# Seven products of sums in place of eight, in the second layer's first product, with second products between them

## The chip, the core and the metric

The kernel runs on one NeuronCore of a Trainium2 chip. The metric is the time of one execution on the device in microseconds (us). Matrix products run on TensorE (PE in the profile, its weight loads PEld), elementwise work on VectorE (DVE), ScalarE (ACT) and GpSimd (POOL); transfers are issued from SyncE's queue (SP).

## What is computed

A linear attention with decay over 2 x 768 tokens of 8 heads of 64, then two feed-forward layers over the 1,536 tokens. The second layer, which the change is about, is a 512 x 2048 product, a leaky relu and a 2048 x 512 product. The weights come as float64.

```python
state = gamma[None, :, None, None] * state + np.einsum('bhd,bhe->bhde', k[:, :, t], v[:, :, t])
y[:, :, t] = scale * np.einsum('bhd,bhde->bhe', q[:, :, t], state)
...
xn = x / rms * rms_g
g = xn @ w_gate
silu = g * (1.0 / (1.0 + np.exp(-g)))
val = xn @ w_val
return (silu * val @ w_out).astype(np.float32)
...
h = x @ w_in
g = np.maximum(0.01 * h, h)
return (g @ w_out).astype(np.float32)
```

## The kernel before

The tokens are cut into three blocks of 512 (`BLOCKS`, numbered 0 to 2), the first layer's 1,536 inner features into 12 blocks of 128, the second's 2,048 into 16. Every operand of a large product is kept as a high part and a low part (`split`, L412 and L413, for what is computed; the conversion of the weights, L362 to L376), and a product is taken as high by high, low by high and high by low. So `product_t` (L407), which multiplies a weight block of 512 x 128 by a token block, is 4 parts of the 512 times 3, that is 12 matrix instructions of 128 x 128 by 128 x 512. A second product (`proj`, L453, in the first layer, `down`, L514, in the second) is 12 too: four output banks times 3.

**Weights.** A block of weights is called a unit: `g`, `v`, `o` of the first layer, `i` and `p` of the second. `fetch` (L342) loads its float64 bits (512 KB), and six steps convert it: three instructions on ACT (L362, L363, L373) and five on DVE (L381, L382, L366, L372, L376). The units come in the order of use, `i` and `p` in turn. There are places for 12 units, and for 10 more once the attention's buffers are given back. After each step of the program `convert` puts 4 or 8 of these conversion steps into it; `need` puts in all that a step's weights still lack.

**The first stage.** The attention goes over 12 chunks of 128 tokens. Per chunk there are scores `sc` (L148), their decay `a` on DVE (L154), an outer product `u` (L164) and heads `y` (L181, L192). Per pair of chunks a norm follows: `tot` on PE (L227), `na` on DVE (L236), a Newton iteration of 13 small instructions on POOL (`nr`, `nt`, L241 to L246), `bc` on PE (L252), then `xg` (L269) and `xl` (L275) on DVE and `xh` (L270) on ACT. The first chunks go through ahead of the first layer, in an order written out by hand; the rest is put between the steps of the first layer on blocks 0 and 1, at a rate worked out from the number of tasks left (`attention`, `per`, `credit`).

**The first layer.** In three groups of four feature blocks (`G1`), for each token block: `gate`, `val` and, one step late, `proj`.

**The second layer.** In three groups of 6, 5 and 5 feature blocks (`G2`), for each of the three token blocks: `up` (the first product, 12 matrix instructions, then a leaky relu `la` on ACT, L501, and the split), and `down` two steps late, which sums over the group's blocks into four banks; `evac` adds them to `y2acc` (L532) and, in the last group, writes them out (L535).

A scheduler takes the program as written, places tiles and sets the order on each engine; only the first part of the attention has an order written out by hand. Banks for products come from a pool of four (`ps`, `bank`), the accumulators of second products from four others (`ps_acc`); `scr` has 6 buffers of 128 x 512 for what comes out of the banks.

Of the kernel before, what the change touches and what calls it, by code (L numbers as in the profile page):

```python
# [23 lines left out]
G2 = [6, 5, 5]  # L24
UNITS = 12
UNITS2 = 10
# [4 lines left out]
EARLY_FETCH = 4  # L31
# [5 lines left out]
def chain_kernel(ctx: ExitStack, tc: tile.TileContext, qk_t, kv, w1, w2, mask, qdec, kdec, sdec, rms_g, ident, out):  # L37
# [244 lines left out]
    def attention(c0, due):  # L282
# [19 lines left out]
        for c in range(c0, NCHUNK + 1):  # L302
# [20 lines left out]
    slots = [[units, UNITS, set()]]  # L323
    wq = [(n + str(f), w1[f, :, i, :]) for f in range(NF1) for i, n in enumerate("gvo")]
    wq += [(n + str(f), w2[f, :, i, :]) for f in range(NF2) for i, n in enumerate("ip")]
    index = {key: i for i, (key, _) in enumerate(wq)}
    raw = {}
    fetched = [0]
    converting = []
    started = [0]  # L330

    def release(key, b):
        if b == NB - 1:
            for s in slots:
                s[2].discard(key)

    def fetch():
        if fetched[0] < min(len(wq), started[0] + RAWS):
            key, src = wq[fetched[0]]
# [4 lines left out]
    def start_unit():  # L344
        slot = next((s for s in slots if len(s[2]) < s[1]), None)
        if slot is None or started[0] == len(wq):
            return False
        key = wq[started[0]][0]
# [3 lines left out]
        slot[2].add(key)  # L352
        t = raw.pop(key)
        low, high = t[:, :, 0], t[:, :, 1]
        a = stage.tile([P, 512], F32, tag="a", name=f"wa_{key}")
# [3 lines left out]
        v = nc.vector  # L359
# [62 lines left out]
    def moe1(g, b, fs, steps):  # L422
# [40 lines left out]
        def evac(banks):  # L463
            if g == 0:
                acc[b] = xp.tile([P, 4, T], F32, tag=f"acc{BLOCKS[b]}", name=f"x2acc{b}")
            last = g == len(G1) - 1
            if last:
                x2h[b] = xp.tile([P, 4, T], F32R, tag=f"xh{BLOCKS[b]}", name=f"x2h{b}")
                x2l[b] = xp.tile([P, 4, T], F32R, tag=f"xl{BLOCKS[b]}", name=f"x2l{b}")
            for m in range(4):  # L470
# [5 lines left out]
                if last:  # L476
                    nc.scalar.activation(out=x2h[b][:, m, :], in_=dst, func=AF.Copy)
            if last:
                for m in range(4):
                    nc.vector.tensor_tensor(  # L480
                        out=x2l[b][:, m, :], in0=acc[b][:, m, :], in1=x2h[b][:, m, :].bitcast(F32), op=ALU.subtract
                    )

        for f in fs:
            steps.append((f"g{f}", b, lambda f=f: gate(f)))
            steps.append((f"v{f}", b, lambda f=f: val(f)))
            steps.append((f"o{f}", b, lambda f=f: proj(f)))

    acc2 = {}

    def moe2(g, b, fs, steps):
        T = BLOCKS[b]
        nt = T // P
        prods = {}

        def up(f):
            hb = bank(f"up{f}_{b}")[:, :T]
            product_t(hb, wt[f"i{f}"], x2h[b], x2l[b])
            release(f"i{f}", b)
            a = scratch(f"la{f}_{b}")[:, :T]  # L500
            nc.scalar.activation(out=a, in_=hb, func=AF.Prelu, alpha=0.01)  # L501
            prods[f] = split(a, f"g2_{f}_{b}", T)

        def down(f):
            if f == fs[0]:
                acc["b"] = acc_banks(f"y2_{g}_{b}", nt)
            h, l = prods.pop(f)
            w = wt[f"p{f}"]
            release(f"p{f}", b)
            for m in range(nt):  # L510
# [10 lines left out]
            if f == fs[-1]:  # L521
                evac(acc.pop("b"))

        def evac(banks):
            if g == 0:
                acc2[b] = xp.tile([P, nt, 512], F32, tag=f"acc{BLOCKS[b]}", name=f"y2acc{b}")
            for m in range(nt):
# [9 lines left out]
        for f in fs:  # L537
            steps.append((f"i{f}", b, lambda f=f: up(f)))
            steps.append((f"p{f}", b, lambda f=f: down(f)))


    def in_order(steps, late):

        order, held = [], []
        for s in steps:
            if s[0][0] in "op":
# [3 lines left out]
            while len(held) > late[s[0][0]]:  # L550
# [4 lines left out]
    for groups, moe in ((G1, moe1), (G2, moe2)):  # L555
        base = 0
        for g, n in enumerate(groups):
            for b in range(NB):
                moe(g, b, list(range(base, base + n)), steps)
# [143 lines left out]
```

## Time and profile before

| | us |
|---|---|
| median of 3 runs (646.64 to 647.08) | 646.76 |
| profiled execution, device time | 642.79 |
| span of the profiled execution, first to last instruction | 641.0 |
| TensorE busy in it | 621.2 |
| VectorE busy | 347.8 |
| ScalarE busy | 270.1 |
| GpSimd busy | 67.8 |

The profile is one execution. Its busy times are sums of instructions; a matrix instruction is shown with its pipeline's depth, so two that follow each other overlap in it, and the time of one in a stream is read from start to start. A wait is idle time of an engine with the instruction that ended it.

### The profile page before, as it was taken

The numbers are of one execution on the slowest core, as the hardware profiler recorded it, in microseconds if no ns is written. First come the engines' busy times: TensorE is split into PE (matmuls) and PEld (weight loads), VectorE is DVE, ScalarE is ACT, GpSimd is POOL, SyncE is SP. The second block draws the span as 40 slices with busy tenths as digits, with TensorE's granted clock in tenths as the row PEclk, the third lists the DMA queues.
The fourth block names the chain that finished last, engine by engine and source line by source line (L and its number), as shares of the span: only waits on it lengthen the run. The fifth ranks groups of instructions, "written<-read, shape, count | busy, mean of one in ns | idle before, by whom it ended". The sixth has DMA issues, their size and how long they took to land.

```text
span 641.0 us, 7899 instructions
## 1 busy us (share of the span) xinstructions
PE 621.2 (97%) x3074; PEld 512.2 (80%) x3074; DVE 347.8 (54%) x596; ACT 270.1 (42%) x482; POOL 67.8 (11%) x128
## 2 busy tenths in 40 slices
PE   7988789999999999999999999999999999999997
PEld 5866678878888888888888888888888888888886
DVE  3888997335999926992415996113951212222122
ACT  2556554426677513752314674325752222222220
POOL 4864545210000000000000000000000000000000
PEclk9998999999999999999999999999999999999999
DMA  9754444002545410532000443001300000001011
GB/s 336 267 208 162 147 151 132 1 1 67 164 137 180 132 44 26 172 132 67 0 1 0 146 150 100 1 0 34 130 2 0 1 0 1 2 0 66 0 66 65
DMA packets 15876, 52.74 MB, mean 82 GB/s; under 512 B 2144, under 2 KB 2272, under 8 KB 15840
## 3 DMA queue, kind: packets, MB, share of 16 engines
q1 hardware_dynamic: 15840, 52.25, 24.1%
q8 instruction: 24, 0.39, 0.2%
q14 instruction: 12, 0.10, 0.0%
HBM read 49.09 MB, written 3.15 MB: 81 GB/s over the span
## 4 chain that ended last, share of the span: by engine, by line
PE 89%; DVE 5%; POOL 2%; ACT 2%; issue 1%; DMA 1%; SPq 0%; POOLq 0%; DVEq 0%
PE up L407 20%; PE y L514 20%; PE x L453 15%; PE val L407 15%; PE gate L407 14%; PE y L192 1%; PE y L181 1%; DMA kdec_sb<-in_kdec 1%; PE sc L148 1%; PE u L164 1%; PE tot L227 1%; DVE wa_v L366 0%; DVE xl L275 0%; DVE wa_v L372 0%; DVE y2acc L532 0%
## 5 line engine op out<-in xcount | busy, mean ns | idle before, releaser
L407 PE MATMUL up<-x2h,w_i 128*128 128x512 f32 x384 | 94.8, 389 | 0.0
L501 ACT ACTIVATE la<-up 128x512 f32<-128x512 f32 x48 | 28.6, 596 | 151.5 <-PE up L407 151.4
L407 PEld LDWEIGHTS up<-x2h,w_i 128*128 128x128 f32 x384 | 72.1, 188 | 15.0
L407 PE MATMUL val<-xh,w_v 128*128 128x512 f32 x288 | 72.9, 395 | 3.7 <-DVE a L154 1.7
L407 PE MATMUL gate<-xh,w_g 128*128 128x512 f32 x288 | 72.6, 392 | 2.4 <-ACT w_g L373 1.2
L407 PEld LDWEIGHTS val<-xh,w_v 128*128 128x128 f32 x288 | 54.2, 190 | 15.7 <-ACT sq L206 1.8
L407 PEld LDWEIGHTS gate<-xh,w_g 128*128 128x128 f32 x288 | 53.6, 188 | 14.7 <-ACT w_g L373 2.8
L440 DVE TENSOR_TENSOR a<-val,t 128x512 f32<-128x512 f32 x36 | 24.7, 687 | 57.4 <-PE val L407 57.4
L407 PE MATMUL up<-x2l,w_i 128*128 128x512 f32 x192 | 51.3, 389 | 0.0
L413 DVE TENSOR_TENSOR g_1l<-la,g_1h 128x512 fp32r<-128x512 f32 x16 | 11.1, 692 | 62.9 <-ACT g_1h L412 62.9
L432 ACT ACTIVATE t<-gate 128x512 f32<-128x512 f32 x36 | 21.4, 594 | 54.8 <-PE gate L407 48.5
L407 PEld LDWEIGHTS up<-x2l,w_i 128*128 128x128 f32 x192 | 36.0, 188 | 7.5
L514 PE MATMUL y<-w_p,g_0h 128*128 128x512 f32 x128 | 39.4, 389 | 0.0
L514 PE MATMUL y<-w_p,g_1h 128*128 128x512 f32 x128 | 39.4, 389 | 0.0
L514 PE MATMUL y<-w_p,g_2h 128*128 128x512 f32 x128 | 39.4, 389 | 0.0
L407 PE MATMUL val<-xl,w_v 128*128 128x512 f32 x144 | 39.1, 394 | 0.0
L407 PE MATMUL gate<-xl,w_g 128*128 128x512 f32 x144 | 38.5, 389 | 0.0
L453 PE MATMUL x<-g_0h,w_o 128*128 128x512 f32 x96 | 33.4, 408 | 1.6 <-ACT g_0h L412 1.6
L413 DVE TENSOR_TENSOR g_0l<-la,g_0h 128x512 fp32r<-128x512 f32 x16 | 11.0, 690 | 41.9 <-ACT g_0h L412 41.9
L407 PEld LDWEIGHTS val<-xl,w_v 128*128 128x128 f32 x144 | 27.6, 192 | 5.8
L453 PE MATMUL x<-g_1h,w_o 128*128 128x512 f32 x96 | 31.6, 390 | 0.0
L407 PEld LDWEIGHTS gate<-xl,w_g 128*128 128x128 f32 x144 | 27.0, 188 | 5.7
(119 smaller groups left out, 1103.6 us busy)
## 6 DMA issues: line engine op xcount, KB each, us to landing
raw_i<-in_w SPq DMA_DIRECT2D x16, 512.0 KB, 3.8
raw_p<-in_w SPq DMA_DIRECT2D x16, 512.0 KB, 3.5
qkT<-in_qk_t SPq DMA_DIRECT2D x12, 512.0 KB, 4.7
kv<-in_kv SPq DMA_DIRECT2D x12, 512.0 KB, 5.9
raw_g<-in_w SPq DMA_DIRECT2D x12, 512.0 KB, 3.5
raw_v<-in_w SPq DMA_DIRECT2D x12, 512.0 KB, 3.4
raw_o<-in_w SPq DMA_DIRECT2D x12, 512.0 KB, 3.6
out<-y2acc SPq DMA_DIRECT2D x12, 256.0 KB, 2.1
```

What stands on the lines that cost most here:

```text
L148: nc.tensor.matmul(out=s["sc"][j][:, t], lhsT=k_[r, t], rhs=q_[r, t], start=True, stop=True)
L164: nc.tensor.matmul(out=u[:, t], lhsT=kd[:, t], rhs=s["kv"][:, 1, t], start=True, stop=True)
L181: nc.tensor.matmul(out=y[:, a * CH:(a + 1) * CH], lhsT=state[(c + 1) % 2][:, a, :], rhs=s["qs"][:, a, :], start=(a == 0), stop=False, skip ...
L192: nc.tensor.matmul(out=y[j * D:(j + 1) * D, a * CH:(a + 1) * CH], lhsT=s["kv"][:, 1, e:e + D], rhs=s["a"][j][:, a, :], start=not inter, st ...
L227: nc.tensor.matmul(out=nrm[cs]["tot"][:, i:i + 1], lhsT=part, rhs=ones, start=(j == 0), stop=(j == len(parts) - 1))
L407: nc.tensor.matmul(out=dst, lhsT=lhs, rhs=rhs, start=(n == 0), stop=(n == len(pairs) - 1))
L413: nc.vector.tensor_tensor(out=l[:, :T], in0=x, in1=h[:, :T].bitcast(F32), op=ALU.subtract)
L432: nc.scalar.activation(out=t, in_=gb, func=AF.Silu)
L440: nc.vector.tensor_tensor(out=a, in0=vb, in1=prods[f], op=ALU.mult)
L453: nc.tensor.matmul(out=acc["b"][m][:, :T], lhsT=lhs, rhs=rhs, start=(f == fs[0] and n == 0), stop=(f == fs[-1] and n == 2),)
L501: nc.scalar.activation(out=a, in_=hb, func=AF.Prelu, alpha=0.01)
L514: nc.tensor.matmul(out=acc["b"][m], lhsT=lhs, rhs=rhs, start=(f == fs[0] and n == 0), stop=(f == fs[-1] and n == 2),)
```

## The change

The second layer's first product on token blocks 1 and 2 is no longer computed block by block. Two neighbouring feature blocks f and e = f + 1 form a pair. Weights and tokens are cut into 2 x 2 parts (feature blocks f and e by two halves of the 512; the halves by token blocks 1 and 2), and the four results of 128 x 512 come from 7 products of sums of parts, where there were 8 products of parts (`quad`). A product of parts (`half`) is 2 parts times 3, that is 6 matrix instructions. The results build up in three banks, X, Z and Y. Between the products ACT copies what stands in X or Z into `scr` (`s1`, `s5`, `u2`), products go on adding into the same bank, and DVE adds the copies to the final banks (`added`). Block 0 keeps `up`.

The sums of weights (`s` units, two for a pair) are formed from the converted `i` units by four DVE instructions of 256 columns and split by two on ACT and two on DVE. The sums of tokens (`sums_of_x2`) are formed once, at the end of the first layer.

The order of steps in the second layer is written out: groups of four feature blocks (`G2`), per group four `up` with a second product behind each, then two pairs, with second products put between their seven products. Second products run up to one group behind. The last of a group's second products on block 1, and those on block 2, stand between the next group's steps; what is left at the end comes back to back.

Other edits: the places for units are 12, 2 for all kinds and 8 for the first layer's alone, which are given back at its end (22 in the first layer as before, 14 in the second where there were 22); `scr` has 5 buffers where it had 6; the conversion's buffer `a` has 3 where it had 2; four empty tasks stand ahead of the last norm's `bc`.

```diff
-G2 = [6, 5, 5]
+G2 = [4, 4, 4, 4]
-UNITS2 = 10
+UNITS2 = 2
+UNITS3 = 8
+HOLD = 5
...
+    stage_a = ctx.enter_context(tc.tile_pool(name="stage_a", bufs=3))
...
-    scr = ctx.enter_context(tc.tile_pool(name="scr", bufs=6))
+    scr = ctx.enter_context(tc.tile_pool(name="scr", bufs=5))
...
-                tasks += norm(due)
+                tasks += [lambda: None] * (4 if c == NCHUNK else 0) + norm(due)
...
+            converting.extend([
+                combine(e[:, two], e[:, one], e[:, two], ALU.add),
+                combine(e[:, one], a[:, one], e[:, one], ALU.subtract),
+                high_part(us[1], e),
+                combine(a[:, one], e[:, two], a[:, one], ALU.subtract),
+                combine(a[:, two], a[:, two], a[:, one], ALU.subtract),
+                high_part(us[0], a),
+                low_part(us[1], e, names[1]),
+                low_part(us[0], a, names[0]),
+            ])
...
+        def first(t, in0, in1, h, l):
+            nc.vector.tensor_tensor(out=t, in0=in0, in1=in1, op=ALU.subtract)
+            nc.scalar.activation(out=h, in_=t, func=AF.Copy)
+
+        def second(t, in0, in1, h, l):
+            nc.vector.tensor_tensor(out=l, in0=t, in1=h.bitcast(F32), op=ALU.subtract)
...
+        def half(dst, key, two, x, start):
...
+            for i, part in ((i, slice(k * P, (k + 1) * P)) for i, k in enumerate(ks)):
+                for lhs, rhs in ((w[:, 0, part], h[:, i]), (w[:, 1, part], h[:, i]), (w[:, 0, part], l[:, i])):
+                    nc.tensor.matmul(
+                        out=dst, lhsT=lhs, rhs=rhs, start=(start and n == 0), stop=(n == 5), skip_group_check=True
+                    )
+                    n += 1
...
+            def kept_sum(n, src):
+                q[n] = scratch(f"{n}_{f}")
+                nc.scalar.activation(out=q[n], in_=src, func=AF.Copy)
+
+            def added(key, src, n, a):
+                nc.vector.tensor_tensor(out=a, in0=src, in1=q.pop(n), op=ALU.add)
+                leaky(key, a, a)
...
+            def p1():
+                q["X"] = bank(f"X{f}")
+                half(q["X"], f"i{f}", False, "B11", True)
+                kept_sum("s1", q["X"])
+
+            def p5():
+                q["Z"] = bank(f"Z{f}")
+                half(q["Z"], f"s{e}", True, "T1", True)
+                kept_sum("s5", q["Z"])
+
+            def p6():
+                half(q["X"], f"s{f}", False, "T2", False)
+                kept_sum("u2", q["X"])
+
+            def p2():
+                q["Y"] = bank(f"Y{f}")
+                half(q["Y"], f"i{f}", True, "B21", True)
+                added((f, 1), q["Y"], "s1", scratch(f"la{f}_1"))
+
+            def p7():
+                half(q["X"], f"s{e}", False, "T3", False)
+                added((e, 2), q["X"], "s5", hold((e, 2)))
+
+            def p3():
+                half(q["Z"], f"s{f}", True, "B22", False)
+                added((f, 2), q["Z"], "u2", hold((f, 2)))
+
+            def p4():
+                half(q["X"], f"i{e}", True, "T4", False)
+                leaky((e, 1), q["X"], scratch(f"la{e}_1"))
...
+            return [
+                ((f"i{f}",), p1), ((f"s{e}",), p5), ((f"s{f}",), p6), ((f"i{f}",), p2),
+                ((f"s{e}",), p7), ((f"s{f}",), p3), ((f"i{e}",), p4),
+            ]
...
+            for f in fs[::2]:
+                behind = {2: (3, 5), 3: (3, 5, 6), 4: (1, 3, 5, 6)}.get(len(fill), (1, 3, 4, 5, 6))
+                for n, (keys, step) in enumerate(quad(f)):
+                    put(keys, 1, step)
+                    if n in behind and fill:
+                        put_down(fill.pop(0))
```

**The order on the engines, place 1: the second layer on PE.** In the rows a name is a tile (`up_2` is `up` on block 2, `y_2_1_0` the second product's bank 0 in group 2 on block 1, `w_s` a sum of weights, `th` and `tl` a sum of tokens). Before, in the last group:

```order
L407 MATMUL up_2_4965<-x2h_3425,w_i_3909 128x512 x8
L407 MATMUL up_2_4965<-x2l_3426,w_i_3909 128x512 x4
L514 MATMUL y_2_1_0_4856<-w_p_4155,g_15_1h 128x512 x2
L514 MATMUL y_2_1_0_4856<-w_p_4155,g_15_1l 128x512
L514 MATMUL y_2_1_1_4857<-w_p_4155,g_15_1h 128x512 x2
L514 MATMUL y_2_1_1_4857<-w_p_4155,g_15_1l 128x512
```

Now, the start of the second pair of the third group:

```order
L616 MATMUL X_4584<-x2h_3089,w_i_4071 128x512 x2
L616 MATMUL X_4584<-x2l_3090,w_i_4071 128x512
L616 MATMUL Z_4603<-x2h_3277,w_s_4181 128x512 x2
L616 MATMUL Z_4603<-x2l_3278,w_s_4181 128x512
L616 MATMUL Z_4603<-x2h_3277,w_s_4181 128x512 x2
L616 MATMUL Z_4603<-x2l_3278,w_s_4181 128x512
L616 MATMUL X_4584<-th,w_s_4180 128x512 x2
L616 MATMUL X_4584<-tl,w_s_4180 128x512
L616 MATMUL X_4584<-th,w_s_4180 128x512 x2
L616 MATMUL X_4584<-tl,w_s_4180 128x512
```

Where 12 products into one bank were followed by 12 into others, bank X is now written, read by ACT and written again with one group of six (Z) between. ACT has there, before the copies of X and Z (`s_10`, `u_10`), a conversion step of another weight block (`wb_p`):

```order
L474 ACTIVATE g_9_1h<-la_1_4552 128x512
L425 ACTIVATE wb_p_4829<-raw_p_4631 128x512
L628 ACTIVATE s_10_4591<-X_4584 128x512
L628 ACTIVATE s_10_4610<-Z_4603 128x512
L628 ACTIVATE u_10_4627<-X_4584 128x512
L387 ACTIVATE w_s_4705<-wa_i_4615 128x512
```

Before, ACT has in the second layer only pairs like this one between the conversion steps:

```order
L501 ACTIVATE la_1_4780<-up_1_4767 128x512
L412 ACTIVATE g_11_1h<-la_1_4780 128x512
L501 ACTIVATE la_1_4811<-up_1_4798 128x512
L412 ACTIVATE g_12_1h<-la_1_4811 128x512
L501 ACTIVATE la_1_4850<-up_1_4837 128x512
```

**Place 2: the attention between the first layer's first steps, on PE.** Before, all 12 instructions of the first `proj` (x) and parts of `gate` and `y` stand ahead of these rows:

```order
L407 MATMUL gate_0_659<-xh_430,w_g_577 128x512 x7
L407 MATMUL gate_0_659<-xl_431,w_g_577 128x512 x4
L192 MATMUL y_674<-a_1_555,kv_535 64x128
L252 MATMUL bc_694<-ident_sb,nr_604 128x128 x2
L407 MATMUL val_0_717<-xh_430,w_v_651 128x512 x8
L407 MATMUL val_0_717<-xl_431,w_v_651 128x512 x4
L164 MATMUL u_742<-kv_539,kd_624 128x128 x4
```

Now `gate` comes straight behind the scores, then the same eight `y`, of which the first row here is the last:

```order
L194 MATMUL y_677<-a_1_558,kv_538 64x128
L254 MATMUL bc_697<-ident_sb,nr_607 128x128 x2
L515 MATMUL x_0_0_0_773<-g_0_0h,w_o_567 128x512
L469 MATMUL val_0_720<-xh_433,w_v_654 128x512
L166 MATMUL u_745<-kv_542,kd_627 128x128 x4
L515 MATMUL x_0_0_0_773<-g_0_0l,w_o_567 128x512
L469 MATMUL val_0_720<-xh_433,w_v_654 128x512 x7
L469 MATMUL val_0_720<-xl_434,w_v_654 128x512 x4
```

The first `proj` moved from ahead of `gate` to behind `bc`. On DVE, three conversion steps of the second `gate` unit (`wa_g`) moved ahead of the step `xg` that the first `gate` waits for, before:

```order
L154 TENSOR_TENSOR a_1_465<-sc_1_439,mask_sb 128x512
L269 TENSOR_TENSOR xg_182<-xg_182,bc_467 128x4x128 x2
L275 TENSOR_TENSOR xl_431<-xg_182,xh_430 128x4x128 x4
L382 TENSOR_SCALAR wa_v_345<-wa_v_345 128x512
L366 SCALAR_TENSOR_TENSOR wa_v_345<-raw_v_129,wa_v_345 128x512
```

and now:

```order
L156 TENSOR_TENSOR a_1_468<-sc_1_442,mask_sb 128x512
L443 TENSOR_SCALAR wa_g_578<-wa_g_578 128x512
L444 TENSOR_SCALAR wa_g_578<-wa_g_578 128x512
L428 SCALAR_TENSOR_TENSOR wa_g_578<-raw_g_271,wa_g_578 128x512
L271 TENSOR_TENSOR xg_185<-xg_185,bc_470 128x4x128 x2
```

**Place 3: the last norm's `bc` on PE.** Before, one `gate` lies between `tot` and `bc`:

```order
L227 MATMUL tot_1316<-ones,ss_1193 128x1
L227 MATMUL tot_1316<-ones,ss_1298 128x1
L407 MATMUL gate_1_1336<-xh_697,w_g_753 128x512 x8
L407 MATMUL gate_1_1336<-xl_698,w_g_753 128x512 x4
L252 MATMUL bc_1351<-ident_sb,nr_1320 128x128 x2
```

Now the two `tot` stand directly ahead of the 12 instructions of a `proj`, of which these are the last, so a `proj` and a `gate` lie between:

```order
L515 MATMUL x_0_1_3_1326<-g_0_1h,w_o_567 128x512
L515 MATMUL x_0_1_3_1326<-g_0_1l,w_o_567 128x512
L515 MATMUL x_0_1_3_1326<-g_0_1h,w_o_567 128x512
L469 MATMUL gate_1_1339<-xh_700,w_g_756 128x512 x8
L469 MATMUL gate_1_1339<-xl_701,w_g_756 128x512 x4
L254 MATMUL bc_1354<-ident_sb,nr_1307 128x128 x2
```

## Rows read from the trace of the kernel before

**Rows 1.** The page: busy time by engine, and the granted clock in 40 slices.

```profile
PE 621.2 (97%) x3074; PEld 512.2 (80%) x3074; DVE 347.8 (54%) x596; ACT 270.1 (42%) x482; POOL 67.8 (11%) x128
PEclk9998999999999999999999999999999999999999
```

**Rows 2.** Busy time in stretches, with the first line naming the columns.

```profile
core 0: us, PE busy (x) PEld busy (x) DVE busy (x) ACT busy (x) POOL busy (x), PEclk, DMA share, GB/s
...
50.00:60.00 10.00, 8.38 (x42) 6.33 (x40) 9.24 (x17) 4.35 (x7) 5.39 (x13) 0.83 0.49 161
...
70.00:80.00 10.00, 7.39 (x46) 6.04 (x47) 9.87 (x17) 6.34 (x14) 6.07 (x10) 0.96 0.62 195
80.00:90.00 10.00, 8.82 (x54) 7.22 (x52) 8.52 (x14) 4.61 (x10) 5.23 (x11) 0.86 0.42 156
...
140.00:343.00 203.00, 203.00 (x897) 168.11 (x896) 133.38 (x240) 96.40 (x164) 0.00 (x0) 1.00 0.28 89
...
373.00:630.00 257.00, 257.00 (x1135) 212.82 (x1134) 85.83 (x144) 88.91 (x151) 0.00 (x0) 1.00 0.09 31
```

**Rows 3.** The chain that ended last: start, duration, instructions in a row.

```profile
373.37 5.44 PE up L407 x24
```

**Rows 4.** PE's waits: line waited for, us in total, times, longest.

```profile
PE bc L252 <- POOL nr L246: 1.9, 2, 1.0
...
PE x L453 <- ACT g_0h L412: 1.6, 1, 1.6
...
PE gate L407 <- ACT w_g L373: 1.2, 1, 1.2
...
PE val L407 <- DVE w_v L376: 0.6, 1, 0.6
```

**Rows 5.** Around an `up`'s end, in order of time: start, duration, engine.

```profile
617.77 0.39 PE L407 MATMUL up<-x2l,w_i 128*128 128x512 f32 x1
618.00 0.62 PE L514 MATMUL y<-w_p,g_2h 128*128 128x512 f32 x2
...
618.20 0.60 ACT L501 ACTIVATE la<-up 128x512 f32<-128x512 f32 x1 [4.18 <-PE up L407]
```

**Rows 6.** Groups of instructions: busy us, mean ns of one, idle before.

```profile
L366 DVE SCALAR_TENSOR_TENSOR wa_i<-raw_i,wa_i 128x512 int32<-128x512 int32 x16 | 11.0, 686 | 0.2
...
L362 ACT ACTIVATE wa_i<-raw_i 128x512 f32<-128x512 f32 x16 | 10.8, 672 | 4.5 <-DVE w_i L376 3.8 <-DVE w_v L376 0.8
...
L381 DVE TENSOR_SCALAR wa_i<-wa_i 128x512 f32<-128x512 f32 x16 | 6.8, 424 | 2.6 <-ACT wa_i L362 2.0
...
L243 POOL TENSOR_TENSOR nt<-nr 128x2 f32<-128x2 f32 x18 | 5.2, 287 | 1.4
```

**Rows 7.** PE in the first stage, at a norm, the first `proj` and the last norm.

```profile
37.88 1.09 PE L192 MATMUL y<-a,kv 128*64 128x128 f32 x16
...
48.64 0.50 PE L227 MATMUL tot<-ones,ss 128*128 128x1 f32 x4
...
51.85 1.56 PE L453 MATMUL x<-g_0h,w_o 128*128 128x512 f32 x3 [1.62 <-ACT g_0h L412]
...
65.05 1.16 PE L148 MATMUL sc<-qkT 64*128 64x128 f32 x16
...
126.19 0.50 PE L227 MATMUL tot<-ones,ss 128*128 128x1 f32 x4
...
130.56 0.71 PE L252 MATMUL bc<-ident_sb,nr 128*128 128x128 f32 x4 [0.98 <-POOL nr L246]
```

**Rows 8.** ACT, DVE and POOL in the first stage, in order of time on each.

```profile
51.17 0.63 ACT L412 ACTIVATE g_0h<-a 128x512 fp32r<-128x512 f32 x1 [1.21 <-DVE a L440]
...
36.32 1.29 DVE L269 TENSOR_TENSOR xg<-xg,bc 128x512 f32<-128x512 f32 x2 [0.89 <-PE bc L252]
...
51.06 0.15 DVE L236 TENSOR_SCALAR na<-tot 128x2 f32<-128x2 f32 x1
...
57.29 0.38 POOL L246 TENSOR_TENSOR nr<-nr,nt 128x2 f32<-128x2 f32 x1
```

More of the change, by code (lines that the diff above doesn't have):

```diff
@@ L351, in start_unit @@
         started[0] += 1
[L352 removed]
+        taken[0] += 1
         t = raw.pop(key)
         low, high = t[:, :, 0], t[:, :, 1]
[L355 removed]
+        a = stage_a.tile([P, 512], F32, tag="a", name=f"wa_{key}")
         m = stage.tile([P, 512], I32, tag="b", name=f"wb_{key}")
@@ L466, in evac @@
             last = g == len(G1) - 1
+            parts = range(4)
+            if last and b == 2:
+                parts = range(2, 4)
             if last:
@@ L475, in evac @@
                     nc.vector.tensor_tensor(out=dst, in0=banks[m][:, :T], in1=dst, op=ALU.add)
-                if last:
+                if last and m in parts:
                     nc.scalar.activation(out=x2h[b][:, m, :], in_=dst, func=AF.Copy)
             if last:
-                for m in range(4):
+                for m in parts:
                     nc.vector.tensor_tensor(
@@ L482, in evac @@
                     )
+            if last and b == 2:
+                sums_of_x2()
         for f in fs:
-            steps.append((f"g{f}", b, lambda f=f: gate(f)))
-            steps.append((f"v{f}", b, lambda f=f: val(f)))
-            steps.append((f"o{f}", b, lambda f=f: proj(f)))
+            steps.append(((f"g{f}",), b, lambda f=f: gate(f)))
+            steps.append(((f"v{f}",), b, lambda f=f: val(f)))
+            steps.append(((f"o{f}",), b, lambda f=f: proj(f)))
     acc2 = {}
[L491 to L494, printed above, removed]
-        def up(f):
[L497 to L504, printed above, removed]
+    late = ExitStack()
@@ L521, in down, with evac @@
             if f == fs[-1]:
-                evac(acc.pop("b"))
-        def evac(banks):
+                evac(g, b, acc.pop("b"))
+            at_ = order.index(key)
+            for k in order[at_ + 1:at_ + 3]:
+                if k not in parted and k not in made:
+                    break
+                part(k)
+        def evac(g, b, banks):
             if g == 0:
-                acc2[b] = xp.tile([P, nt, 512], F32, tag=f"acc{BLOCKS[b]}", name=f"y2acc{b}")
-            for m in range(nt):
+                acc2[b] = xp.tile([P, 4, 512], F32, tag="acc512", name=f"y2acc{b}")
+            for m in range(4):
                 dst = acc2[b][:, m, :]
@@ L549, in in_order @@
                 order.append(s)
-            while len(held) > late[s[0][0]]:
+            while len(held) > 1:
                 order.append(held.pop(0))
@@ L554, in chain_kernel @@
     steps = []
[L555 to L559, printed above, removed]
-            base += n
-    steps = in_order(steps, {"g": 1, "v": 1, "o": 1, "i": 2, "p": 2})
+    base = 0
+    for g, n in enumerate(G1):
+        for b in range(NB):
+            moe1(g, b, list(range(base, base + n)), steps)
+        base += n
+    steps = in_order(steps)
+    moe2(steps)
     if True:
@@ L611, in chain_kernel @@
         seen = -1
-        for i, (key, b, step) in enumerate(steps):
-            if b > seen and key[0] == "g":
+        for i, (keys, b, step) in enumerate(steps):
+            if b > seen and keys[0][0] == "g":
                 seen = b
@@ L630, in chain_kernel @@
                 credit -= 1
-            ahead = max([index[k] for k, _, _ in steps[i:i + 4]], default=0)
+            ahead = max([index[k] for ks, _, _ in steps[i:i + 4] for k in ks if k in index], default=0)
             pace = PACE if started[0] > ahead else 2 * PACE
-            convert(pace)
+            if sums:
+                sums.pop(0)()
+            else:
+                convert(pace)
 def kernel(**inputs):
```

155 lines of the change are left out of this document (133 added, 22 removed).

## The prediction

> **What bounds the kernel now.** I read the busy times first: TensorE is busy 621.2 of 641.0 us [rows 1]. The stretches say where the rest lies: from 140 to 343 us and from 373 to 630 us it is busy all the time at full clock (2.4 GHz, granted 1.00), while VectorE works 133 of 203 us and 86 of 257 us [rows 2]. The chain of waits names matrix instructions there, 24 in 5.44 us [rows 3]: 0.2267 us each, start to start. So in the second layer a matrix instruction less is 0.2267 us less, as long as nothing makes TensorE wait. What TensorE loses lies ahead of 140 us, where the attention is worked in between the first layer's steps: VectorE is the full engine (9.24 and 9.87 us of 10), TensorE waits, and the clock falls for a while to 1.2 GHz (means of 0.83, 0.96 and 0.86) [rows 2], which costs 1.7, 0.4 and 1.4 us, since a mean of 0.83 over 10 us is 3.4 us at half speed.
>
> **Products removed.** For a pair of feature blocks, blocks 1 and 2 took 4 times 12 matrix instructions; now they take 7 times 6. That is 6 fewer in each of 8 pairs, 48 in all, of the same shape: 48 x 0.2267 = **-10.9 us**, with no doubt about the count. The second products are as many as before. The Trainium skill, "TensorE: Matmul & The Clock Gate", section "Back-to-back issue gap", gives about 131 ns for a 512-column instruction in a sustained stream and about 216 ns for an isolated one; by those the 48 would be worth 6.3 or 10.4 us. The rows say 227 ns over whole stretches of this kernel, and the rows decide.
>
> **Elementwise work added.** Per pair: sums and splits of weights (6 DVE, 2 ACT), copies out of the banks (3 ACT), additions (3 DVE); once, the sums of tokens (8 DVE instructions of twice the length, 4 ACT). At 0.69 us for the longest DVE form of 512 columns and 0.67 for ACT [rows 6] that is at most 8 x 9 x 0.69 + 8 x 1.4 = 61 us of DVE and 8 x 5 x 0.67 + 4 x 1.3 = 32 us of ACT. The second layer leaves DVE 171 us and ACT 168 us idle in 257 [rows 2]. The 14 places for units in place of 22 also push conversions out of the first layer: before, 18 units of the second layer were ready at its first `up`; now it is 9 and 4 sums. The nine that move cost DVE 9 x 2.9 = 26 us. So DVE rises from 86 to about 170 us of some 246, a load of 70%: taken at **0**. Without that cover it would be paid where a pair begins before its sums stand; in the order the sums of weights stand up to a group ahead (some 60 us), and those of tokens some 40 matrix instructions (9 us) ahead of their use.
>
> **Waits added.** Bank X is written, read and written again. How long that takes: from the start of the last matrix instruction to the start of ACT's read 618.20 - 617.77 = 0.43 us [rows 5], the read 0.60 [rows 5], and from its end to TensorE's start 51.85 - (51.17 + 0.63) = 0.05 [rows 7, 8]: 1.08 us. With a group of six between, TensorE wants to go on 7 x 0.2267 = 1.59 us after the start of that last instruction. The margin is 0.51 us. In the order this tight case stands at six places: before the third product (copy `s1`) in the second pair of each of the four groups, and before the fifth (copy `u2`) and the seventh (an addition on DVE, 0.69, margin 0.42) in the very first pair. At every other place a second product (2.72 us) or more lies between. One instruction in front on the reading engine (0.67) makes 0.2 to 0.3 us of wait, two make 0.8. A seventh tight place is the seam between the layers, where the last two `proj` now follow each other and the second needs what three instructions on DVE and ACT make of `val` (0.43 + 3 x 0.69 = 2.5 against 13 x 0.2267 = 2.95). Bounds 0 and 7 x 0.8 = 5.6; I take **+0.5**, because little but conversion steps can be in front, and ACT, at 89 + 32 and some 18 us of moved conversions in 246, is idle four tenths of the time.
>
> **The first stage, which the other edits reorder.** Three terms.
> (a) The last `bc` waited 0.98 us [rows 7]: it could go 130.56 - 126.19 = 4.37 us after `tot`. Now 24 matrix instructions lie between, 5.44 us, enough even if `na` stands behind one DVE instruction: **-1.0** (to 0).
> (b) Place 2. The wait of 1.62 us for the first `proj`'s input, and the 1.7 us of low clock behind it [rows 2, 4, 7], have 12 `gate` instructions ahead of them now. But `bc` now stands 1.1 + 2.7 + 1.0 us of work behind `tot` (scores, `gate`, `y`), and its input was ready 57.67 - 49.14 = 8.5 us behind it: 1.9 to `na`, 6.6 on POOL [rows 7, 8]. A new wait of up to 3.7 us. TensorE does the same work up to the next scores in either order, so I follow the new order to there, with 1.0 us of delay from the conversion steps that went ahead of `xg`: `bc` at 57.7 + 1.0 = 58.7, 0.7 for itself [rows 7], then on DVE the first `xg` and the last step of `w_v` (1.3) to 60.7, 11 instructions of `val` to 63.2, 10 of `proj` to 65.5, where the trace has 65.05: **+0.4**. If POOL's 13 instructions ran at their mean of 0.287 us (3.7, not 6.6) it would be -2.5. The three conversion steps are 0.42 + 0.42 + 0.69 = 1.5 us against 0.89 us of idle time [rows 6, 8], 0.6 us of delay at least; for the upper end I take twice their length, 2 us more than the 1.0 above, and 1.7 for a fall of the clock at the new wait: +4.1.
> (c) The rest to 107 us. The waits for `w_g` (1.2) and `w_v` (0.6) [rows 4] end about a dozen matrix instructions earlier in the order, and by the end of the stretch DVE has done four conversion steps more (72 against 68, 2.2 us) on an engine that is full: -1.8 to +2.2, I take **-1.0**.
>
> **The end** is as before: the last second product, four additions, four writes. **Sum:** -10.9 + 0.5 - 1.0 + 0.4 - 1.0 = **-12.0 us**. On the profiled execution, 642.8 us (its span and 1.8 around it), that is 630.8. The median of the runs is 4.0 us above that execution, which no row explains; I let it stand and forecast 646.8 - 12.0 = **634.8 us**, 1.9% less.
>
> **The rivals.** (1) The first stage gets worse: the new wait at `bc` comes whole, with a fall of the clock (+4.1 in place of +0.4): 638.5. For it speaks that DVE is full there and has more in front; against, that the old order paid two waits and a fall at the same place. (2) The first stage gets better: the low-clock stretches go with the waits (b at -2.5, c at -1.8, and 0.4 + 1.4 of clock at 70 to 90 us): 634.8 - 5.5 = 629.3, or half of it, 632. (3) Sums of weights late, so that the pairs do not run as written: one DVE instruction of 0.69 for each of 8 pairs is +5.5, 640.3; the order speaks against it. (4) Slower. Waits at bank X in each pair make the clock fall. In the rows a wait of 1.62 us stands before a stretch that lost 1.7 us [rows 2, 4]; a wait of 0.8 and such a stretch for each of 8 pairs is +20: 654. It makes the kernel slower from 12.0 / 8 = 1.5 us for a pair. Against it: the margins above, and that the kernel already turns over four banks with 12 instructions each at a clock of 1.00 from 373 to 630 us [rows 2]. The Trainium skill, the same page, section "A second HAM failure mode: psum-queue depth-cycling", tells of a kernel of 512-column instructions in which turning over banks left short idle times that made the clock swing; no row of the second layer here shows that, and the groups are now half as long.
>
> **How the numbers follow.** Forecast 0.58, (1) 0.16, (2) 0.14, (3) 0.05, (4) 0.04, and 0.03 that several small losses together use up the gain. What a measurement here can tell from no change is about 0.2%, 1.3 us. The range goes from 630.5 (most of 2) to 640.5 (1 with some wait in the pairs, and 3). Faster 0.93, same 0.03, slower 0.04.
>
> **What would show it.** Right: 48 fewer matrix instructions; TensorE without idle time from the last `bc` to the end but for a few waits of `X` on ACT or DVE of under 0.5 us; clock 1.00 there; the stretch from the first `up` to the last second product 10 to 11 us shorter; no wait at the last `bc`. Wrong: a wait at the second `bc` beyond 4 us; waits of products on `w_s` or `th`; a fall of the clock inside the pairs.

## The result, and the profile after

| us | before | after |
|---|---|---|
| median of 4 runs each | 646.7 (645.0 to 647.1) | 630.4 (629.8 to 631.2) |
| profiled execution, device time | 642.79 | 631.17 |
| its span | 641.0 | 629.4 |

The ratio is 0.9754, 95% interval 0.9732 to 0.9775. The forecast was 634.8 (630.5 to 640.5): faster, as forecast, but by 16.3 us of the medians where 12.0 were forecast, and 0.1 us under the range. On the two profiled executions the difference is 11.6.

Of the page after: busy time by engine, and the granted clock in 40 slices.

```profile
PE 612.3 (97%) x3026; PEld 505.6 (80%) x3026; DVE 400.1 (64%) x686; ACT 296.3 (47%) x524; POOL 68.2 (11%) x128
PEclk9799999999999999999999999999999999999999
```

TensorE has 3026 matrix instructions where it had 3074 [rows 1], 48 fewer. Busy time in stretches (columns as in [rows 2]):

```profile
20.00:30.00 10.00, 10.00 (x76) 9.26 (x74) 8.00 (x14) 4.36 (x10) 7.29 (x17) 0.67 0.54 209
50.00:60.00 10.00, 7.31 (x57) 5.82 (x56) 7.57 (x16) 7.37 (x14) 5.39 (x16) 1.00 0.37 127
...
373.00:620.00 247.00, 247.00 (x1091) 204.55 (x1090) 154.39 (x261) 126.68 (x213) 0.00 (x0) 1.00 0.14 47
```

In the second layer TensorE is busy throughout, at a clock of 1.00, with VectorE at 154 of 247 us, where it had 86 of 257 [rows 2]. The fall of the clock at 50 to 60 us [rows 2] is gone; another one, at 20 to 30 us, is there that the profiled execution of before did not have.

The first and the last matrix instructions of the second layer, after (start, duration):

```profile
375.01 1.98 PE L469 MATMUL up<-x2h,w_i 128*128 128x512 f32 x8
...
625.02 0.39 PE L692 MATMUL y<-w_p,g_2l 128*128 128x512 f32 x1
```

From the first start to the last end that is 250.40 us. Before, the first `up` starts at 373.20 and the last product ends at 637.21: 264.01 us, with the last `proj` of the first layer (2.72) in it, so 261.29. The second layer is 10.89 us shorter.

In the first stage, TensorE at the `bc` of place 2, at the scores behind it, and at the last norm, after:

```profile
59.87 0.71 PE L254 MATMUL bc<-ident_sb,nr 128*128 128x128 f32 x4 [1.21 <-POOL nr L248]
...
66.95 1.16 PE L150 MATMUL sc<-qkT 64*128 64x128 f32 x16
...
123.79 0.50 PE L229 MATMUL tot<-ones,ss 128*128 128x1 f32 x4
...
129.73 0.61 PE L254 MATMUL bc<-ident_sb,nr 128*128 128x128 f32 x4
```

They answer to [rows 7]. The two spans, cut at five instructions of TensorE:

| stretch, us | before | after | difference | forecast |
|---|---|---|---|---|
| start to the scores at 65 | 65.05 | 66.95 | +1.90 | +0.4 (b) |
| to the last scores, at 104 | 38.74 | 37.27 | -1.47 | -1.0 (c) |
| to block 1's first `gate`, at 107 | 3.29 | 3.20 | -0.09 | |
| to the second layer, its last `proj` counted ahead of it | 268.84 | 267.59 | -1.25 | -1.0 (a) |
| the second layer | 261.29 | 250.40 | -10.89 | -10.4 |
| the end | 3.79 | 3.99 | +0.20 | 0 |

### The profile page after: what moved, and what is told of

Same layout as the page of the kernel before. It is cut to its first block, busy times and chain, and to the rows that moved or that the text cites. A ratio compares the mean times of both kernels' runs of the same rounds, so it can differ in the third digit from the quotient of the medians.

```text
span 629.4 us, 7975 instructions
## 1 busy us (share of the span) xinstructions
PE 612.3 (97%) x3026; PEld 505.6 (80%) x3026; DVE 400.1 (64%) x686; ACT 296.3 (47%) x524; POOL 68.2 (11%) x128
## 4 chain that ended last, share of the span: by engine, by line
PE 87%; DVE 8%; issue 1%; POOL 1%; DMA 1%; ACT 1%; SPq 0%; DVEq 0%; POOLq 0%
PE y L692 20%; PE val L469 15%; PE x L515 14%; PE gate L469 14%; PE X L616 7%; PE up L469 7%; PE Z L616 3%; PE Y L616 2%; PE y L194 1%; PE sc L150 1%; PE y L183 1%; PE u L166 1%; PE tot L229 1%; DMA kdec_sb<-in_kdec 1%; DVE xg L271 1%
## 5 line engine op out<-in xcount | busy, mean ns | idle before, releaser
L469 PE MATMUL val<-xl,w_v 128*128 128x512 f32 x144 | 38.7, 391 | 0.0
L715 DVE TENSOR_TENSOR y2acc<-y,y2acc 128x512 f32<-128x512 f32 x36 | 23.6, 687 | 16.5 <-PE y L692 16.5
L515 PE MATMUL x<-g_0h,w_o 128*128 128x512 f32 x96 | 31.9, 393 | 0.0
L469 PE MATMUL up<-x2h,w_i 128*128 128x512 f32 x128 | 31.6, 389 | 0.0
L515 PE MATMUL x<-g_2h,w_o 128*128 128x512 f32 x96 | 31.3, 389 | 0.0
L469 PEld LDWEIGHTS up<-x2h,w_i 128*128 128x128 f32 x128 | 24.0, 188 | 5.0
L692 PEld LDWEIGHTS y<-w_p,g_0h 128*128 128x128 f32 x128 | 24.0, 188 | 5.0
L692 PEld LDWEIGHTS y<-w_p,g_2h 128*128 128x128 f32 x128 | 24.0, 188 | 5.0
L692 PEld LDWEIGHTS y<-w_p,g_1h 128*128 128x128 f32 x128 | 24.0, 188 | 5.0
```

The source lines that it names most:

```text
L469: nc.tensor.matmul(out=dst, lhsT=lhs, rhs=rhs, start=(n == 0), stop=(n == len(pairs) - 1))
L515: nc.tensor.matmul(out=acc["b"][m][:, :T], lhsT=lhs, rhs=rhs, start=(f == fs[0] and n == 0), stop=(f == fs[-1] and n == 2),)
L692: nc.tensor.matmul(out=acc["b"][m], lhsT=lhs, rhs=rhs, start=(f == fs[0] and n == 0), stop=(f == fs[-1] and n == 2),)
L715: nc.vector.tensor_tensor(out=dst, in0=banks[m], in1=dst, op=ALU.add)
```

## The experiments

Each was timed beside the kernel before: medians of it 645.0 in the first four, 644.9 in the second four, 644.4 in the last.

**e1: the kernel before, once more.** 

> The kernel before, unchanged, so that each run's span and mean granted clock are seen, not the time alone. Open is why its runs take 645.0 to 647.1 us where its profiled execution took 642.8. Theory A (the prediction's: the 4 us are a cost that every run of every kernel has outside the span): span near 641 at a clock of 0.995, and a time some 5 us longer than the span. Theory B (the first stage loses more in most executions than in the profiled one): spans of 643 to 645 us, each some 1.8 us below its time, and a clock below 0.995.

Its 12 runs take 641.6 to 646.8, each 1.8 us above its own span (639.8 to 645.0), at clocks of 0.988 to 0.997. What lies between median and profiled execution lies inside the span: theory B. It is 2.2 us by the 27 runs of before timed beside these four (median 645.0), not 4.0: the other 1.7 were the draw of the first runs. The profiled execution of this set has a span of 644.2. It reaches the scores at 65 us 1.2 us later, with a fall of the clock between 8 and 16 us ahead of them. From those scores to the last it takes 40.87 us, against 38.74. There a load came late. The rows of it, ScalarE, TensorE, then SyncE's queue and GpSimd:

```profile
94.98 0.66 ACT L363 ACTIVATE wb_g<-raw_g 128x512 int32<-128x512 uint32 x1 [2.65 <-DMA raw_g<-in_w]
95.55 0.58 ACT L432 ACTIVATE t<-gate 128x512 f32<-128x512 f32 x1
...
96.18 2.83 PE L407 MATMUL val<-xh,w_v 128*128 128x512 f32 x8 [2.49 <-ACT t L432]
...
88.11 0.33 SPq L96 DMA_DIRECT2D qkT<-in_qk_t  x1
...
89.94 0.37 SPq L342 DMA_DIRECT2D raw_g<-in_w  x1
...
83.96 2.88 POOL L246 TENSOR_TENSOR nr<-nr,nt 128x2 f32<-128x2 f32 x1
86.79 1.29 POOL L130 TENSOR_TENSOR qs<-qkT,qdec_sb 128x512 f32<-128x512 f32 x1
```

Read from below: an instruction of GpSimd on 128 x 2 elements took 2.88 us; `qs` behind it was late; so was the load into the buffer that `qs` frees (85.62 in the first execution); and `raw_g`, behind that load and one of `kv` on SyncE's queue, went out at 89.94, where the first execution shows 86.53. ScalarE waited 2.65 us for it with the silu `t` behind, and TensorE 2.49 us for `t`. After, `raw_g` stands ahead of that load, and goes out at 81.50:

```profile
81.50 0.33 SPq L356 DMA_DIRECT2D raw_g<-in_w  x1
86.24 0.33 SPq L98 DMA_DIRECT2D qkT<-in_qk_t  x1
```

**e2: the side edits alone**, on the kernel before: `scr` 5, `stage_a` 3, the four empty tasks; on TensorE the first stage has the order of after.

```diff
-    scr = ctx.enter_context(tc.tile_pool(name="scr", bufs=6))
+    scr = ctx.enter_context(tc.tile_pool(name="scr", bufs=5))
+    stage_a = ctx.enter_context(tc.tile_pool(name="stage_a", bufs=3))
...
-                tasks += norm(due)
+                tasks += [lambda: None] * (4 if c == NCHUNK else 0) + norm(due)
```

> The kernel before with the edits of the first stage alone (3 buffers a, 5 buffers scr, the empty tasks); the second layer keeps its eight products. Theory A (the prediction's sum): -1.0 + 0.4 - 1.0 = -1.6 us against before. Theory B (what the medians show beyond the 10.9 us of the products, 16.3 - 10.9, is won in the first stage): -5 us. Rival: the side edits are worth nothing, and the products more than counted: 0.

640.9 (639.9 to 641.6), ratio 0.9938 (0.9918 to 0.9958): -4.2 us, near theory B. The ten runs lie within 1.7 us, where the 27 of before spread over 5.9; e4 and e5, which have the same side edits, spread over 4.2 and 4.1.

**e3: after with two buffers `a`.** 

> The kernel after with two buffers a, which gives the order of the first stage as it was before up to the last norm; the seven products stay. Theory A: -10.9 + 0.5 - 1.0 = -11.4 us against before, 0.6 slower than after. Theory B: as A against before, but 4 to 5 us slower than after, since the first stage is the old one. Rival: the third buffer is needed by the sums of weights, and their conversion holds up pairs: waits of products on w_s, 1 us or more for each.

632.0, from 629.4 to 635.0, ratio 0.9807 (0.9773 to 0.9842): 2.2 above after's 629.8 (e5), between A and B, but the interval overlaps that of e5, and its fastest run is as fast as after's. The times alone do not show what the third buffer is worth by itself. No product waited for `w_s`, and the second layer takes 250.41 us. From block 1's first `gate` to the second layer it is 1.2 us shorter than before, as after and e2 are. These three share the empty tasks and the five buffers `scr`, which no run parts; the wait that is gone, at the last `bc`, stands where the empty tasks were put. On TensorE the order up to the last scores is that of before, and the profiled execution has the loss of e1, larger: TensorE waits 3.9 us for `t`, and it is 43.29 us from the scores at 65 to the last.

**e4: eight products in the new order.** Four plain `up` for a pair in place of the seven, no sums.

```diff
+            return [((f"i{k}",), lambda k=k, b=b: up2(k, b)) for k, b in ((f, 1), (e, 1), (f, 2), (e, 2))]
```

> The kernel after with eight products in place of seven on blocks 1 and 2, with no sums of weights or tokens, in the same groups and with second products between them; the first stage is that of after. Theory (48 matrix instructions at 0.2267 us, all else at nothing): 10.9 us slower than after, 641.3. If the elementwise work that the seven products add costs TensorE time, the difference is smaller; if the new grouping helps by itself, this kernel is faster than before by more than the side edits alone.

640.7 (ratio 0.9953, 0.9931 to 0.9976). The rows of its second layer:

```profile
373.59 1.98 PE L469 MATMUL up<-x2h,w_i 128*128 128x512 f32 x8
...
634.48 0.39 PE L627 MATMUL y<-w_p,g_2l 128*128 128x512 f32 x1
```

That is 261.28 us, against 261.29 before and 250.40 after: the new groups and order are worth nothing by themselves, and the 48 instructions 10.88 us, which is 48 x 0.2267.

**e5: after, once more.** 

> The kernel after, unchanged, on the chip of the next three. The runs so far give before 645 us with its first stage at a clock of 0.987 to 0.997, and 640.9 for before with the side edits. Theory (48 matrix instructions at 0.2267 us with nothing taken back): 10.9 below the side edits, 630.0, and about 15 below before, spread no wider than 2 us. If the third buffer makes the early clock falls rarer, its runs lie closer together than those of before.

629.8 (629.3 to 633.4), ratio 0.9780 (0.9752 to 0.9808). Two of its six runs are 2 and 4 us above the rest, so the spread is not below 2 us as expected.

**e6: loads of the last chunks from GpSimd's queue**, on the kernel before.

```diff
-            nc.sync.dma_start(out=a, in_=qk_t[c])
+            (nc.gpsimd if c >= 10 else nc.sync).dma_start(out=a, in_=qk_t[c])
```

(and the same for `kv`.) 

> The kernel before, with the loads of the last two chunks (qkT and kv) issued from GpSimd's queue in place of SyncE's; the order on TensorE, VectorE and ScalarE is that of before. Theory: before's bad executions lose 3.3 us between 85 and 110 us, because the load of a gate unit (raw_g) stands behind those of a chunk on SyncE's queue, which wait for GpSimd's qs; ScalarE then waits 2.6 us for raw_g with the silu of the gate behind it, TensorE waits 2.5 us for that, and the clock falls. With the chunk's loads elsewhere raw_g goes out 3 to 4 us earlier: the wait for the silu is gone, and the median is 2 to 3 us under that of before. Rival: the loss comes from the early clock falls (8 to 30 us) or from VectorE's load, whatever the loads do: no change, within 0.5 us.

645.8 (643.6 to 647.4), ratio 1.0017 (0.9996 to 1.0038): no gain. TensorE's wait for `t` is gone from the profile, but the stretch from the scores at 65 us to the last takes 41.22 us all the same, with waits for `w_v` (1.7), `w_g` (1.3) and `ss` (1.2). So the late load is one form of the loss and not its cause. VectorE in that stretch, in before, e1, e3, then after, e5 (columns as in [rows 2], each from its scores at 65 to 67 us to its last):

```profile
65.05:103.79 38.74, 33.69 (x230) 27.19 (x229) 37.01 (x56) 20.26 (x41) 20.10 (x28) 0.96 0.46 149
```

```profile
66.27:107.14 40.87, 35.14 (x230) 28.35 (x229) 36.65 (x58) 20.21 (x41) 22.92 (x28) 0.92 0.43 142
```

```profile
64.86:108.15 43.29, 36.33 (x229) 29.28 (x228) 36.70 (x59) 20.23 (x41) 22.99 (x28) 0.88 0.41 134
```

```profile
66.95:104.22 37.27, 33.46 (x230) 27.65 (x229) 36.50 (x60) 19.83 (x40) 20.30 (x28) 0.95 0.49 169
```

```profile
67.01:103.28 36.27, 32.05 (x229) 26.66 (x228) 35.94 (x61) 20.15 (x41) 20.44 (x27) 1.00 0.52 174
```

VectorE has 36 to 37 us of work there in each, and is idle 1.7, 4.2 and 6.6 us in the old order, 0.8 and 0.3 in the new (0.3 to 1.2 over all eight profiles that have it): the stretch takes what VectorE needs and what it is kept idle. In e6, old order too, it is idle 1.7 us, and its instructions themselves take 39.5. That VectorE bounds the stretch is read from these rows; no run gave it more work there.

**e7: the third product directly behind the first.** 

> The kernel after with the third product of each pair (into X, behind the copy s1) directly behind the first (into X), and the second product (into Z) after it: at eight places no group of six lies between. Theory: TensorE waits 0.43 + 0.60 + 0.05 - 0.23 = 0.85 us at each of the eight, 6.8 us slower than after, more where a conversion step is in front on ScalarE, with the clock at 1.00. Rival (the prediction's fourth): such waits make the clock fall, another 1.7 us for each, 20 us slower than after in all.

632.8, but the second layer takes 251.22 us, 0.82 more than after; the rest is the first stage. The scheduler did not keep the order: at each of the eight places it put four instructions of another product between. TensorE and, below, ScalarE at one of them:

```profile
409.28 0.39 PE L616 MATMUL X<-x2l,w_i 128*128 128x512 f32 x1
409.51 0.62 PE L616 MATMUL Z<-x2h,w_s 128*128 128x512 f32 x2
409.96 0.39 PE L616 MATMUL Z<-x2l,w_s 128*128 128x512 f32 x1
410.19 0.39 PE L616 MATMUL Z<-x2h,w_s 128*128 128x512 f32 x1
410.48 0.73 PE L616 MATMUL X<-th,w_s 128*128 128x512 f32 x2
...
409.29 0.66 ACT L424 ACTIVATE wa_p<-raw_p 128x512 f32<-128x512 f32 x1
409.85 0.58 ACT L628 ACTIVATE s<-X 128x512 f32<-128x512 f32 x1
```

Four instructions and a wait of 0.06 us are all that the turn of X needs here, with a conversion step in front of the copy. The price of a turn with nothing between was not measured.

**e8: all second products behind the pair.**

```diff
-                    if n in behind and fill:
-                        put_down(fill.pop(0))
+                    for _ in range(len(behind) if n == 6 else 0):
+                        if fill:
+                            put_down(fill.pop(0))
```

> The kernel after with the second products of each pair all behind its seven products, not between them: 24 places (three for a pair) have only one group of six between a bank's last write and its next, a margin of 0.42 to 0.51 us. Theory (the margin holds as long as the reading engine is free): 0 to 2 us slower than after, with waits of 0.2 to 0.3 us where a conversion step is in front. Rival (second products between are needed as cover, one instruction of 0.67 in front everywhere): 24 x 0.25 = 6 us slower; with two in front, 19 us.

628.8 (628.0 to 631.0), ratio 0.9757 (0.9730 to 0.9784), no different from e5 by the intervals. The order held (X, Z, X, Y, X, Z, X in all eight pairs), and the second layer takes 250.54 us: 24 tight places cost 0.14 us together.

**e9 and e10: more work for VectorE.** The last conversion step four and six times.

```diff
+                    for _ in range(4):
                         v.tensor_tensor(out=u[:, 1, :], in0=x, in1=u[:, 0, :].bitcast(F32), op=ALU.subtract)
...
+            for _ in range(4 if key[0] in "ip" else 1):
                 v.tensor_tensor(out=u[:, 1, :], in0=a, in1=u[:, 0, :].bitcast(F32), op=ALU.subtract)
```

> The kernel after with the last conversion step on VectorE (the low part of i, p and s units) issued four times over, same result each time: about 24 us of VectorE work more in the second layer for each repetition, so 154 + 72 = 226 of 247 us, and half as much again in the first layer. Theory (the cover of the elementwise work is free as long as VectorE does not run full): the second layer, from the first up to the last second product, stays at 250.4 us within 1. Rival (VectorE's queue makes the tight places wait): 24 tight or nearly tight places at 0.3 us or more, 257 us or more.

> As the run before it, with six times: 154 + 121 = 275 us of VectorE work against 247 of TensorE, more than fits. Theory: VectorE becomes the bound, the second layer takes 275 to 285 us, TensorE waits for sums of weights and for additions. It shows too whether such waits make the clock fall there: if they do, as the fourth rival of the prediction has it, the granted clock in the second layer is under 0.97; if not, it is 1.00.

e9 (two runs): 631.2, second layer 250.62 us. e10 (one run): 665.3, second layer 285.56 us. The second layer of e9 in one stretch, and a part of it:

```profile
373.00:620.00 247.00, 247.00 (x1091) 204.25 (x1090) 211.21 (x368) 126.35 (x213) 0.00 (x0) 1.00 0.15 48
...
430.00:580.00 150.00, 150.00 (x663) 124.23 (x662) 149.09 (x270) 81.22 (x140) 0.00 (x0) 1.00 0.18 57
```

and of e10 two waits of TensorE and three stretches:

```profile
524.36 1.79 PE L694 MATMUL y<-w_p,g_2l 128*128 128x512 f32 x4 [2.26 <-DVE g_2l L477]
531.08 1.22 PE L618 MATMUL Z<-x2h,w_s 128*128 128x512 f32 x2 [4.93 <-ACT s L630]
...
490.00:500.00 10.00, 8.04 (x36) 6.27 (x35) 10.00 (x19) 5.21 (x10) 0.00 (x0) 1.00 0.15 48
520.00:530.00 10.00, 3.89 (x14) 2.34 (x12) 10.00 (x19) 3.78 (x7) 0.00 (x0) 0.74 0.23 75
530.00:540.00 10.00, 6.39 (x14) 4.61 (x15) 10.00 (x18) 3.56 (x6) 0.00 (x0) 0.50 0.25 82
```

With VectorE at 211 of 247 us, 86%, TensorE still never waits, and the mean hides the better part: from 430 to 580 us VectorE is full (149.09 of 150 us), and TensorE does not wait there either. So the busy share alone does not set the limit; how far ahead of their use the results must stand was not measured. In e10, with more work than fits, TensorE stands still for up to 5.1 us at a time. A wait of 1.96 us at 495 left the clock at 1.00. Behind the one of 2.26 us, which ended at 524.36, it fell to half (1.2 GHz) within a microsecond, ahead of the one of 4.93, and stayed there past 540. The mean from 374 to 660 us is 0.95, under the 0.97 that was named for such a fall.

**e11 and e12: four buffers `a`**, with four `hold`; e12 with the order of e8 too.

> The kernel after with four buffers a in place of three (and four hold buffers in place of five, for room). Theory: between the scores at 65 us and those at 104 us VectorE is the bound; with two buffers it idles 1.4 to 6.6 us there, with three 0.3 to 0.8, so a fourth has nothing left to win: within 0.5 us of after, 629.8. Rival (each buffer more gives conversions a longer lead, which TensorE's waits of about 3 us in that stretch still want): 1 to 3 us faster than after.

> The kernel after with its second products behind the pairs (as in the run that took 628.8 us) and four buffers a: the fastest version that the runs point to. Theory (neither is worth anything beyond the second layer's 250.4 us): 628.8 to 629.8 us. If the order of second products is worth something by itself, it lies 1 us under the run with four buffers.

633.4 (ratio 0.9827, 0.9797 to 0.9858) and 632.0 (0.9804, 0.9771 to 0.9838): both medians above after's 629.8, where the same time was expected, with intervals that overlap that of e5. The second layers are as they were (250.40 and 250.63). In the profile of e11 the stretch to the last scores is 37.26 us, as in after, but a wait of 1.7 us for `ss` stands ahead of them and the clock falls behind it: 4.80 us from there to block 1's first `gate`, where after has 3.20. It is not a matter of four buffers alone: the profile of e7, with three, has a wait of 2.3 us for `ss` there, and 4.79 us behind it. Whether four buffers meet it more often was not settled. No version here is shown to beat after.

## Why the prediction was right, and where it was wrong

**The products** were right: 10.9 forecast, 10.88 by e4. **The elementwise work at 0** was right: VectorE at 154 of 247 us (forecast: 170 of 246), and e9 puts the end of the cover beyond 211.

**The waits at bank X** were 0, not 0.5. One tight place of after, TensorE and, below, ScalarE:

```profile
407.42 0.39 PE L616 MATMUL X<-x2l,w_i 128*128 128x512 f32 x1
407.65 0.62 PE L616 MATMUL Z<-x2h,w_s 128*128 128x512 f32 x2
...
409.01 0.62 PE L616 MATMUL X<-th,w_s 128*128 128x512 f32 x2
...
407.43 0.66 ACT L424 ACTIVATE wa_p<-raw_p 128x512 f32<-128x512 f32 x1
408.00 0.58 ACT L628 ACTIVATE s<-X 128x512 f32<-128x512 f32 x1
```

The copy starts 0.58 us after the last start, where 0.43 is the least, and ends at 408.58, 0.43 us ahead of TensorE's next start. The step that failed is "One instruction in front on the reading engine (0.67) makes 0.2 to 0.3 us of wait". By the margin that stands beside it, it is 0.67 - 0.51 = 0.16 us for ScalarE at most, and only if the conversion starts as late as it can. Here it started with the product's last instruction (407.43) and held the engine 0.57 us, of which 0.43 would have passed anyway: it uses 0.15 of the 0.51 us. That is the only one of the five tight copies that a conversion held up; at the other four ScalarE was free and the copy started 0.43 us after the last start. Among e8's copies of X the latest starts 0.80 us after the last start, still without a wait of TensorE. No product waited for `w_s` or `th` either. So rivals 3 and 4 fall, and with them the range's upper end. The Trainium skill, "TensorE: Matmul & The Clock Gate", section "A second HAM failure mode: psum-queue depth-cycling", which stands beside rival 4, tells of short idle times between groups of matrix instructions. They did not arise here: TensorE is busy for all of 247 us at a clock of 1.00, with a bank turned over every six instructions. So this kernel does not test what they would do to the clock.

**(a)** was right: -1.0 forecast, -1.25 measured, and e3 has it too. The wait of 0.98 us at the last `bc` is gone; 0.27 us more than that is not explained.

**(b)** was too low: +0.4 forecast, +1.9 measured, inside the bounds of -2.5 to +4.1. The loss stands ahead of place 2, at the first `gate`. TensorE there before, after and in e8, then VectorE after:

```profile
35.57 0.71 PE L252 MATMUL bc<-ident_sb,nr 128*128 128x128 f32 x4 [0.90 <-POOL nr L246]
38.90 2.14 PE L407 MATMUL gate<-xh,w_g 128*128 128x512 f32 x8
...
36.66 0.71 PE L254 MATMUL bc<-ident_sb,nr 128*128 128x128 f32 x4 [0.50 <-POOL nr L248]
41.70 2.11 PE L469 MATMUL gate<-xh,w_g 128*128 128x512 f32 x8 [1.47 <-ACT xh L272]
...
35.61 0.71 PE L254 MATMUL bc<-ident_sb,nr 128*128 128x128 f32 x4 [0.89 <-POOL nr L248]
40.66 2.14 PE L469 MATMUL gate<-xh,w_g 128*128 128x512 f32 x8 [1.47 <-ACT xh L272]
...
36.44 0.45 DVE L443 TENSOR_SCALAR wa_g<-wa_g 128x512 f32<-128x512 f32 x1
36.91 1.36 DVE L444 TENSOR_SCALAR wa_g<-wa_g 128x512 int32<-128x512 int32 x1
38.31 1.42 DVE L428 SCALAR_TENSOR_TENSOR wa_g<-raw_g,wa_g 128x512 int32<-128x512 int32 x1
39.65 1.27 DVE L271 TENSOR_TENSOR xg<-xg,bc 128x512 f32<-128x512 f32 x2
```

The `bc` comes 1.1 us later after a stretch at half speed (23 to 30 us); e8, which has the order of after and no such fall, has it at 35.61. From there to `gate` it is 5.04 us (5.05 in e8) where it was 3.33: the three conversion steps ahead of `xg` took 3.2 us, not the 1.5 of the sum, the last two of them beside GpSimd's `qs` and `kd` (36.56 to 39.18). So the term that was mis-sized is the delay from them, taken as 1.0 us: it is 1.7. From `tot` to the scores place 2 then took 15.40 us against 16.41, with its `bc` at 59.87, not 58.7, and a wait of 1.21 us, not 3.7. That gain is the clock's and not the order's: e1 and e3 have the old order and its wait for the first `proj` (1.69 and 1.66) at a clock of 1.00, and take 15.28 and 15.26 us. An early fall of the clock, somewhere between 8 and 38 us, is in 12 of the 14 profiles; the kernel before had been profiled in one without. Over executions the scores come at 65.5 us in the old order (4 profiles) and at 66.7 in the new one (8): +1.2.

**(c)** is the term that was mis-sized most, and behind it the step that failed: "the median of the runs is 4.0 us above that execution, which no row explains; I let it stand". I took the 4 us for a cost of every run, so that they stayed in the forecast. Of them 1.7 were luck of the draw (646.7 in the first runs, 645.0 in the 27 timed beside e1 to e4). The other 2.2 are the first stage's, and the side edits take them away: the median of e2 lies 0.4 us under its own profiled execution. From the scores at 65 us to the last the old order takes 38.7, 40.9, 41.2 and 43.3 us, the new one 35.9 to 37.5: -4.3 in the mean, where the one profile of before, the shortest of the four, left room for -1.5. With it the terms close: +1.2 - 4.3 - 1.25 = -4.4 us for the first stage, against -4.2 in e2, and -15.3 with the products, against -15.1 on the chip of e5 and -16.3 in the first runs. So the first stage gave some 4.4 us where 1.6 were forecast, and that puts the time at the lower end of the range. The nearest rival is 2 (629.3, with 0.14): its gain in the stretch of (c), in part by less low clock (0.95 to 1.00 after, 0.88 to 0.96 before), came; its gain at (b) did not.

How the third buffer does it is shown in part. That it is this edit rests on the orders: with two buffers (e3) the old order is back. VectorE, which is nearly full in that stretch, stands idle less; in e1 and e3 the late `raw_g` on SyncE's queue is one way in which it came to stand idle. That only this rank did it was the guess of e6, and fell. I counted conversion steps on VectorE for the upper bound of (c), and did not follow the queue of loads past which they had moved.

## What to carry to other kernels

A matrix instruction saved in a stretch where TensorE never waits was worth its whole issue time here, even though the saving is paid in elementwise work. What to ask of the paying engine is whether TensorE waits for it, not its busy share: in e9 VectorE was full for 150 us and TensorE did not wait. A bank could be read and written again behind one group of six 512-column instructions (1.59 us from start to start), with a conversion step in front of the read. A step of VectorE costs what it takes beside GpSimd's work, which was two to three times its length elsewhere (1.36 and 1.42 us against 0.42 and 0.69). A gap between the profiled execution and the median is a question to the spans of the other runs before it is a constant: it may sit in the very stretch that an edit touches.

## What the hardware showed

An instruction of GpSimd on 128 x 2 elements, mostly 0.2 to 0.5 us, took 2.88 in e1 and in e3, while VectorE worked without a gap from 83.89 to 86.78 us in e1, on six instructions of 0.40 to 0.67 us, three of them with two inputs in SBUF. What held it is not shown: VectorE had worked without a gap for some 4 us before that too, and the same GpSimd instructions took 0.19 to 0.53 there. The other way round, a VectorE instruction of 0.67 us took 1.77 in the first profile of before, to the moment at which GpSimd's `qs` ended and 0.5 us more. The Trainium skill, "SBUF — State Buffer", section "SBUF: two separate sides", says that one pair of ports is shared, and that an instruction of GpSimd, or one of VectorE with two inputs in SBUF, whichever starts first, has it for its whole length while the other waits. The 1.77 us agree with that. The 2.88 us are longer than any of the six, so that one such turn does not explain them.
